# Phase 1 of a fused attention and two-MLP kernel: four engines pinned to the text's order, the attention cut into a table of half units

## Chip, core and metric

One core of a Trainium2 chip runs the whole program. The metric is the device time of one execution in microseconds; lower is better.

## What is computed

```python
# q, k, v: 8 batches x 8 heads x 576 positions x 64; together 4608 tokens of 512 columns
q_s = exp(q - max(q, -1));  q_s /= sum(q_s, -1) + 1e-9
k_s = exp(k - max(k, 2));   k_s /= sum(k_s, 2) + 1e-9
x = einsum(q_s, einsum(k_s, v))                  # linear attention, then heads to columns
x = relu(x @ w_in) ** 2 @ w_out                  # phase 1: 512 -> 2048 -> 512
xn = x / sqrt(mean(x * x) + 1e-6) * rms_g        # phase 2: 512 -> 1536 -> 512
out = (silu(xn @ w_gate) * (xn @ w_val)) @ w_out2
```

The weights come as 64-bit floats and are converted on the chip.

## The kernel before

**Tiles.** The 4608 tokens are nine blocks of 512 (`NB`). Phase 1 goes over the blocks, and in each over sixteen chunks of 128 of the 2048 hidden columns (`FF1`). One block and chunk (j, c) is a **unit**. Every matmul operand is split into a high and a low part, so that a product is three matmuls (`PASSES`): high times high, high times low, low times high.

**A unit** is twelve matmuls into `ps_h` (`p1_h`, through `mm3`, L107), then on ACT a Relu (L625), a Square (L626) and the copy of the high part (L78), on DVE the subtraction that leaves the low part (L79, `g<-r,g`), and two units later (`LAG`) twelve matmuls into the four accumulators `acc` (`p1_B`, L107). The first product of the second half of block 1's chunks is made in block 0 already (`kept`, `AHEAD`), so that the second eight units of block 1 have only the `acc` matmuls. The last unit of a block is followed by four copies of `acc` to `e` (L663 on DVE, L665 on ACT) and four stores.

**The attention** of the next block runs beside these units, one pair of heads (`hp`, four of them) after the other. For each pair PE makes a transpose `ps_kt` (L453), a second one `ps_kb` (L464), four transposes `ps_q` (L540), twenty small matmuls `ps_kv` (L558) and six matmuls `ps_x` (L107). All five take their bank from two (`a0`, `a1`, in turn): the next one can start when the tile before the last has been read.

```python
return ps_a.tile([P, 512], F32, tag=f"a{turns['a'] % 2}", name=name)   # a_ps
```

Between them stand DVE and ACT steps: the maximum over k (`mk`, L441 and L444), `mc` and `mcb` out of `ps_kt` (L455, L457; `ps_kb` transposes `mcb`), the subtraction from k out of `ps_kb` (L474), its exponential `ke` (L494), the same for q (`qm` L503, `qt` L510, L514), its sum and quotient (`qs` L518 to L520, `qn` L527), the high and low part of `qT` out of `ps_q`, `rk` and `kvf` out of `ps_kv` (L574 to L578), and the two parts of `kvd` and of `x`, the latter out of `ps_x`. The parts go through `split`: high on ACT (L78), low on DVE (L79).

**Weights.** Those of phase 1 are converted during block 0, and written to DRAM but for eight tiles; a ring of seven tiles (`ws`) is filled again from there by SP. Those of phase 2 are converted in blocks 2 to 6, by `tick`: a load of 64-bit words (`raw`), a word on POOL (`s<-raw`, L242) and one on ACT (L245), three instructions on DVE (L257, L265, L269, called a **conversion** below), then sums (L329) and low parts (L274) on POOL, the high part on ACT (L273), and a store that ACT's queue issues.

**Order.** The text gives each unit its products, then the ticks that are due, then the attention steps that `A_STEPS` and `A_STARTS` put on this unit. Most instructions may be moved by the scheduler of the program's layer, engine by engine, by priority; only those wrapped in `held` keep their place in the text (the first instruction of each PE step of the attention, and the high parts on ACT).

Of the kernel before, what the change touches and what calls it, by code (L numbers as in the profile page):

```python
# [22 lines left out]

@with_exitstack
def attention_moe_kernel(
# [12 lines left out]
    nc = tc.nc  # L38
    B, H, S, D = q.shape
# [34 lines left out]
    def held(j, ins):  # L74
        return tc.keep_in_program_order(ins) if j > 0 else ins

    def split(dst, src, j=0):
        held(j, nc.scalar.activation(out=dst[:, 0], in_=src, func=AF.Copy))  # L78
        nc.vector.tensor_tensor(  # L79
            out=dst[:, 1], in0=src, in1=dst[:, 0].bitcast(F32), op=ALU.subtract  # L80
        )

    def split_by_pe(dst, ps, j):
        held(j, nc.scalar.activation(out=dst[:, 0], in_=ps, func=AF.Copy))
        nc.tensor.matmul(ps, neg_r, dst[:, 0], start=False, stop=True, skip_group_check=True)
# [147 lines left out]
    def d_words(key):  # L233
# [5 lines left out]
        if key[0] in ("i", "o"):  # L239
            nc.scalar.activation(out=s, in_=hi, func=AF.Copy, scale=2.0**-112)  # L240
        else:
            nc.gpsimd.tensor_scalar(  # L242
                out=s, in0=hi, scalar1=2.0**-112, scalar2=0.0, op0=ALU.mult, op1=ALU.add
            )
        nc.scalar.activation(out=n, in_=r[:, :, 0], func=AF.Copy, scale=2.0**-29)  # L245
        words[key] = s, n

    def d_float(key):
# [8 lines left out]
        nc.vector.tensor_scalar(  # L257
# [7 lines left out]
        nc.vector.scalar_tensor_tensor(  # L265
# [15 lines left out]
    def flush(all=False):  # L281
        for x in late:
            x[0] -= 1
        while late and (late[0][0] < 0 or all):
            _, key, t = late.pop(0)
            if key[0] not in PROD:
                tc.keep_in_program_order(nc.scalar.dma_start(out=wd[key], in_=flat(t)))
                continue
            for g in range(2):
# [3 lines left out]
                    nc.scalar.dma_start(  # L293
# [24 lines left out]
    def d_quad(key):  # L318
# [7 lines left out]
        def d_sum(name, in0, in1, op):  # L326
            def run():
                f[name] = pools["q"].tile([P, 512], F32, tag=name, name=name, bufs=1)
                nc.gpsimd.tensor_tensor(out=f[name], in0=f[in0], in1=f[in1], op=op)  # L329
# [90 lines left out]
    def a_loadv(j, hp):  # L420
# [4 lines left out]
        nc.gpsimd.memset(vt[:, :, :, D : D + 1], 1.0)  # L425
# [10 lines left out]
    def a_kmax(j, hp):  # L436
# [23 lines left out]
    def a_kb(j, hp):  # L460
# [3 lines left out]
        held(j, nc.tensor.transpose(ps[:, 0:P], mcs.pop((j, hp)), ident))  # L464
        mcs[j, hp] = ps

    def a_ksub(j, hp):
# [4 lines left out]
        for rows, cs in k_parts:  # L472
            n = cs.stop - cs.start
            nc.vector.tensor_tensor(  # L474
# [12 lines left out]
    def a_kexp(j, hp):  # L487
# [5 lines left out]
        for rows, cs in k_parts:  # L493
            ins = nc.scalar.activation(out=ke[rows, cs], in_=kv_[rows, cs], func=AF.Exp)  # L494
# [6 lines left out]
    def a_qmax(j, hp):  # L501
        qm = pools["a"].tile([P, 2 * NG], F32, tag="qm", name="qm")
        nc.vector.reduce_max(out=qm, in_=q_heads(j, hp), axis=AX.X)  # L503
        qms[j, hp] = qm

    def a_qsub(j, hp):
        qv = q_heads(j, hp)
        qm = qms.pop((j, hp)).unsqueeze(2).to_broadcast([P, 2 * NG, D])
        eng = nc.vector if j > 0 else nc.gpsimd
        eng.tensor_tensor(out=qv, in0=qv, in1=qm, op=ALU.subtract)  # L510

    def a_qexp(j, hp):
        qv = q_heads(j, hp)
        held(j, nc.scalar.activation(out=qv, in_=qv, func=AF.Exp))  # L514

    def a_qsum(j, hp):
        qs = pools["a"].tile([P, 2 * NG], F32, tag="qs", name="qs")
        nc.vector.reduce_sum(out=qs, in_=q_heads(j, hp), axis=AX.X)  # L518
        nc.vector.tensor_scalar_add(out=qs, in0=qs, scalar1=1e-9)
        nc.vector.reciprocal(out=qs, in_=qs)  # L520
        qms[j, hp] = qs

    def a_qn(j, hp):
# [3 lines left out]
        nc.vector.tensor_tensor(  # L527
# [7 lines left out]
    def a_qT(j, hp):  # L535
        ps = a_ps(j, hp, "ps_q")
        qt = qns.pop((j, hp))
        for c in range(NG):
            src = qt[:, c].rearrange("p h d -> p (h d)")
            ins = nc.tensor.transpose(ps[:, c * P : (c + 1) * P], src, ident)  # L540
            if c == 0:
                held(j, ins)
        qT = a_tile(j, hp, [2, T], "qT", F32R)
# [4 lines left out]
        qTs[j, hp] = qT  # L548

    def a_kv(j, hp):  # L550
# [18 lines left out]
    def a_kvd(j, hp):  # L569
        if j >= B:  # L570
# [15 lines left out]
        split(kvd[j % 2][hp], f, j)  # L586
# [5 lines left out]
    def a_x(j, hp):  # L592
        ps = a_ps(j, hp, "ps_x")
        qT = qTs.pop((j, hp))
        xts[j, hp] = xp.tile([P, 2, T], F32R, tag="x", name="x")
# [15 lines left out]
        if j < 2:  # L611
            split_by_pe(xts[j, hp], ps, j)
        else:
            split(xts[j, hp], ps, j)
# [5 lines left out]
    def p1_h(j, c, pool, bufs):  # L620
        ps = ps_h.tile([P, T], F32, tag="h", name="ps_h")
        for kk in range(KD):
            mm3(ps, wl(("i", c), kk), lambda b: xts[j, kk][:, b, :], kk == 0, kk == KD - 1)
        r = pool.tile([P, T], F32, tag="r", name="r", bufs=bufs)
        nc.scalar.activation(out=r, in_=ps, func=AF.Relu)  # L625
        nc.scalar.activation(out=r, in_=r, func=AF.Square)  # L626
        return r

    def p1_A(j, c):
        if ahead(j, ("i", c)):  # L630
            r = kept.pop(c)
        else:
            r = p1_h(j, c, gp, 2)
# [17 lines left out]
    def p1_B(j, c):  # L651
# [7 lines left out]
        if c == FF1 - 1:  # L659
# [426 lines left out]
```

## Time and profile before

| | |
|---|---|
| Median of 3 runs | 1773.79 us (1771.77 to 1775.23) |
| The profiled execution | 1773.63 us, of it the profile's span 1771.5 us |
| PE busy | 1718.5 us, 97% of the span |
| DVE, ACT, POOL busy | 1086.5 us (61%), 761.8 us (43%), 154.9 us (9%) |
| Chain that ended last | PE 71%, DMA 4%, DVE, POOL and ACT 1% each |

The span is that of the instructions on the core; some 2 us of the execution lie outside it. Busy time is the sum of the instructions' own times. PE overlaps matmuls, so a group of twelve is best read from the start of one group to the start of the next.

### The profile page before, as it was taken

What the parts mean: (1) busy time and instruction counts of PE and PEld (TensorE: products, weight loads), DVE (VectorE), ACT (ScalarE), POOL (GpSimd) and SP (SyncE); (2) the same over time, 40 slices, a digit from 0 to 9 for tenths busy, and PEclk for the clock granted to TensorE, in tenths of its full rate; (3) what the DMA queues carried; (4) which work ended last, traced back from release to release, by engine and by line L of the source; (5) the groups of instructions that cost most, each with busy time, mean ns of one, the idle gap of its engine ahead of it and who ended that gap; (6) DMA issues with size and microseconds to landing.
All of it is one profiled execution on the core that took longest, in us unless ns stands there. A gap on an engine that the chain in (4) does not pass through costs nothing.

```text
span 1771.5 us, 22992 instructions
## 1 busy us (share of the span) xinstructions
PE 1718.5 (97%) x8338; PEld 1417.2 (80%) x8338; DVE 1086.5 (61%) x1866; ACT 761.8 (43%) x1351; POOL 154.9 (9%) x166
## 2 busy tenths in 40 slices
PE   5899998999998999999999999999999999999998
PEld 3678877887886888888888888888888888888997
DVE  7987576555587445332275777667757775756444
ACT  5677435444555444443445334423442343223221
POOL 2000035013165002010000000000000000000000
PEclk9999998999999999999999999999999999999999
DMA  6788658678799557565556557666666566666885
GB/s 184 242 276 287 217 190 282 209 226 291 221 369 314 181 185 238 168 206 194 190 166 226 191 190 252 202 212 200 236 216 216 192 215 219 199 209 195 287 298 204
DMA packets 184511, 398.41 MB, mean 225 GB/s; under 512 B 57424, under 2 KB 96336, under 8 KB 183248
## 3 DMA queue, kind: packets, MB, share of 16 engines
q1 hardware_dynamic: 156368, 356.05, 61.5%
q10 hardware_dynamic: 28032, 40.90, 6.4%
q8 instruction: 67, 1.10, 0.3%
q14 instruction: 44, 0.36, 0.1%
HBM read 337.12 MB, written 59.77 MB: 224 GB/s over the span
## 4 chain that ended last, share of the span: by engine, by line
PE 71%; DMA 4%; DVE 1%; POOL 1%; ACT 1%; issue 0%; SPq 0%; ACTq 0%; POOLq 0%
PE acc L107 28%; PE ps_h L107 12%; PE ps_y L792 8%; PE ps_v L792 8%; PE ps_x L792 8%; PE ps_w L792 4%; DMA wd_t<-so 1%; DMA raw<-in_w_gv 1%; PE ps_x L107 1%; DMA ws<-wd_o 1%; PE ps_kv L558 1%; DMA wd_u<-so 0%; POOL so L274 0%; PE ps_q L540 0%; DMA raw<-in_w_out 0%
## 5 line engine op out<-in xcount | busy, mean ns | idle before, releaser
L107 PE MATMUL ps_h<-x,ws 128*128 128x512 f32 x1296 | 326.5, 402 | 4.0 <-DVE ws L274 2.6
L107 PE MATMUL acc<-g,ws 128*128 128x512 f32 x1296 | 313.9, 391 | 1.6 <-DVE g L79 1.1
L107 PE MATMUL acc<-ws,g 128*128 128x512 f32 x1296 | 313.4, 390 | 1.0 <-ACT g L78 0.9
L79 DVE TENSOR_TENSOR g<-r,g 128x512 fp32r<-128x512 f32 x252 | 180.0, 714 | 214.0 <-ACT g L78 212.0
L107 PEld LDWEIGHTS ps_h<-x,ws 128*128 128x128 f32 x1296 | 242.1, 191 | 58.2 <-DVE ws L274 3.9
L107 PEld LDWEIGHTS acc<-g,ws 128*128 128x128 f32 x1296 | 243.2, 188 | 54.3 <-DVE g L79 2.0
L107 PEld LDWEIGHTS acc<-ws,g 128*128 128x128 f32 x1296 | 241.4, 188 | 51.4 <-ACT g L78 2.1
L78 ACT ACTIVATE g<-r 128x512 fp32r<-128x512 f32 x252 | 158.8, 630 | 252.7 <-DVE r L831 225.7
L625 ACT ACTIVATE r<-ps_h 128x512 f32<-128x512 f32 x144 | 85.3, 593 | 212.2 <-PE ps_h L107 202.8
L792 PE MATMUL ps_y<-xo,ws 128*128 128x512 f32 (+1 forms) x720 | 168.7, 369 | 0.0
L792 PE MATMUL ps_v<-xo,ws 128*128 128x512 f32 (+1 forms) x720 | 168.5, 368 | 0.0
L792 PE MATMUL ps_x<-xo,ws 128*128 128x512 f32 (+1 forms) x720 | 167.4, 368 | 0.0
L792 PEld LDWEIGHTS ps_x<-xo,ws 128*128 128x128 f32 x720 | 128.0, 188 | 23.5
L792 PEld LDWEIGHTS ps_v<-xo,ws 128*128 128x128 f32 x720 | 127.7, 188 | 23.4
L792 PEld LDWEIGHTS ps_y<-xo,ws 128*128 128x128 f32 x720 | 126.4, 189 | 24.2 <-DVE sa L704 1.5
L107 PE MATMUL ps_h<-x,w 128*128 128x512 f32 x432 | 110.0, 402 | 1.7 <-DVE w L274 0.9
L107 PE MATMUL acc<-g,w 128*128 128x512 f32 x432 | 104.2, 390 | 1.0 <-ACT w L273 1.0
L107 PEld LDWEIGHTS ps_h<-x,w 128*128 128x128 f32 x432 | 80.6, 192 | 20.5 <-DVE w L274 1.3
L107 PEld LDWEIGHTS acc<-g,w 128*128 128x128 f32 x432 | 80.9, 188 | 18.3 <-ACT w L273 1.4
L626 ACT ACTIVATE r<-r 128x512 f32<-128x512 f32 x144 | 90.0, 629 | 12.8 <-POOL so L274 8.7
L808 DVE TENSOR_TENSOR u<-ps_y,p 128x512 f32<-128x512 f32 (+1 forms) x120 | 76.1, 634 | 23.3 <-PE ps_y L792 21.6
L819 ACT ACTIVATE sg<-silu 128x512 f32<-128x512 f32 (+1 forms) x90 | 51.4, 585 | 81.4 <-DVE silu L808 78.8
(113 smaller groups left out, 1852.8 us busy)
## 6 DMA issues: line engine op xcount, KB each, us to landing
ws<-wd_t SPq DMA_DIRECT2D x210, 512.0 KB, 4.1
ws<-wd_u SPq DMA_DIRECT2D x108, 512.0 KB, 4.2
ws<-wd_o SPq DMA_DIRECT2D x96, 512.0 KB, 4.1
ws<-wd_i SPq DMA_DIRECT2D x89, 512.0 KB, 4.2
wd_t<-so ACTq DMA_DIRECT2D x84, 256.0 KB, 5.0
raw<-in_w_out SPq DMA_DIRECT2D x28, 512.0 KB, 5.2
raw<-in_w_gv SPq DMA_DIRECT2D x24, 512.0 KB, 6.0
x2d<-e SPq DMA_DIRECT2D x36, 256.0 KB, 3.2
```

The lines of the kernel that those rows point to most:

```text
L78: held(j, nc.scalar.activation(out=dst[:, 0], in_=src, func=AF.Copy))
L79: nc.vector.tensor_tensor(out=dst[:, 1], in0=src, in1=dst[:, 0].bitcast(F32), op=ALU.subtract)
L107: ins = nc.tensor.matmul(ps, lhsT(a), rhs(b), start=first and n == 0, stop=last and n == 2, skip_group_check=part,)
L558: ins = nc.tensor.matmul(ps[h * D : (h + 1) * D, 0 : D + 1], ke[0:m, c, h, :], vt[0:m, c, h, :], start=c == 0, stop=c == SF,)
L625: nc.scalar.activation(out=r, in_=ps, func=AF.Relu)
L626: nc.scalar.activation(out=r, in_=r, func=AF.Square)
L792: nc.tensor.matmul(ps, w[:, q % 2, o : o + P], x(xa, kk), start=first and kk == 0 and m == 0, stop=last and kk == 1 and m == 2, skip_group ...
L808: nc.vector.tensor_tensor(out=out, in0=in0, in1=in1, op=ALU.add)
L819: nc.scalar.activation(out=g, in_=h, func=AF.Sigmoid)
```

## The change

From the second block to the last but one (`FF1 <= i < n1 - FF1`, 112 of the 144 units) every instruction of VectorE, ScalarE, GpSimd and TensorE is kept in the text's order: `ve`, `se`, `ge` and `te` wrap the engines and do this while `pinned[0]` is set. SP's queue is not wrapped. The text of these units is written anew:

- A unit has two halves. The first is the `ps_h` matmuls of unit i, then ACT's Relu, Square and high part of unit i-1, then the attention steps of half 2i. The second is the `acc` matmuls of unit i-2, DVE's low part of unit i-1, the tick and one POOL output if due, then the steps of half 2i+1.
- The attention of blocks 2 to 8 is the table `HALVES`: 23 steps, each with its half relative to the pair's start; pairs follow each other every eight halves. `split` is cut into `split_hi` (ACT) and `split_lo` (DVE), which have a half each, and so have `a_kt` and `a_mc`, `a_kb` and `a_ksub`, `a_kv` and `a_kvf`. Block 1's attention stays as it was.
- The copies of `acc` to `e` (`p1_out`) move to the third unit of the next block, ahead of its attention steps; that unit has no `acc` matmuls, as before, and the fourth has two sets.

No instruction is added or left out: on each engine there are as many of each kind as before. Block 8 and phase 2 have the order that they had.

```diff
+class InOrder:
+    def __getattr__(self, name):
+        f = getattr(self.engine, name)
+        def call(*args, **kw):
+            ins = f(*args, **kw)
+            return self.tc.keep_in_program_order(ins) if self.on[0] else ins
+        return call
...
+    ve, se, ge, te = (
+        InOrder(tc, engine, pinned) for engine in (nc.vector, nc.scalar, nc.gpsimd, nc.tensor)
+    )
...
-    A_STEPS = ((-5, a_loadk), (-4, a_loadq), (0, a_qmax), (0, a_kmax), (1, a_qsub), (1, a_ktr))
-    A_STEPS += ((3, a_kbs), (2, a_qexp), (3, a_loadv), (3, a_qsum), (4, a_kexp))
-    A_STEPS += ((4, a_qn), (6, a_kvn), (6, a_qT), (8, a_x))
-    A_STARTS = {1: (-6, -4, -2, 0), 2: (-6, -3, 0, 3)}
...
+    HALVES = ((-12, a_loadk), (-10, a_loadq), (-3, a_kmax), (-2, a_qmax), (0, a_qsub))
+    HALVES += ((0, a_loadv), (2, a_qexp), (3, a_kt), (3, a_qsum), (4, a_mc), (4, a_qn))
+    HALVES += ((6, a_kb), (7, a_ksub), (8, a_kexp), (8, a_qT), (9, a_qT_hi), (10, a_qT_lo))
+    HALVES += ((10, a_kv), (11, a_kvf), (12, a_kvd_hi), (13, a_kvd_lo), (14, a_x))
+    HALVES += ((15, a_x_hi), (16, a_x_lo))
...
+                    at += (j - 1) * 2 * FF1 - 11 + 2 * FF1 // NP * hp
...
+            pinned[0] = FF1 <= i < n1 - FF1
...
             p1_A(j, c)
+            if not pinned[0]:
+                p1_hi(j, c)
+                p1_lo(j, c)
+            for x in last:
+                p1_hi(*x)
+            if pinned[0] and c == LAG:
+                p1_out(j - 1)
+            attention(2 * i)
             pending.append((j, c, None))
             while len(pending) > (LAG + 1 if j > 0 and c == LAG else LAG):
                 p1_B(*pending.pop(0)[:2])
+            for x in last:
+                p1_lo(*x)
+            last = [(j, c)] if pinned[0] else []
             while ticks[0] < n_ticks(i):
                 tick()
             if i > 2 * FF1 and outs:
                 outs.pop(0)()
...
-            for n, ja, hp, f in todo.get(i, ()):
-                f(ja, hp)
+            attention(2 * i + 1)
```

**Where the order moves.** PE at the start of block 2 (`w_655` is a resident tile of the second unit's weights), before:

```order
L540 MATMUL ps_q<-ident,qn 128x128 x4
L558 MATMUL ps_kv<-vt,ke 64x65 x10
L107 MATMUL ps_h<-x,w_655 128x512 x12
L107 MATMUL acc_2102<-g,w_1944 128x512 x3
L107 MATMUL acc_2103<-g,w_1944 128x512 x3
L107 MATMUL acc_2104<-g,w_1944 128x512 x3
L107 MATMUL acc_2105<-g,w_1944 128x512 x3
L464 MATMUL ps_kb<-ident,mcb 128x128
L107 MATMUL ps_h<-x,ws 128x512 x12
L107 MATMUL ps_x<-qT,kvd_0_84 128x4x48 x3
```

and with the change (all lines of wrapped calls read L34):

```order
L34 MATMUL ps_h<-x,w_655 128x512 x12
L34 MATMUL acc_2100<-g,w_1961 128x512 x3
L34 MATMUL acc_2101<-g,w_1961 128x512 x3
L34 MATMUL acc_2102<-g,w_1961 128x512 x3
L34 MATMUL acc_2103<-g,w_1961 128x512 x3
L34 MATMUL ps_x<-qT,kvd_0_84 128x4x48 x3
L34 MATMUL ps_x<-qT,kvd_0_88 128x4x80 x3
L34 MATMUL ps_kb<-ident,mcb 128x128
L34 MATMUL ps_h<-x,ws 128x512 x12
L34 MATMUL ps_q<-ident,qn 128x128 x4
L34 MATMUL ps_h<-x,ws 128x512 x12
```

`ps_q` and `ps_kv` stood between `ps_kt` and `ps_kb` and took the two banks; now `ps_x` and `ps_kb` follow each other behind the `acc` group, and `ps_q` stands one unit later.

DVE in block 2 before, from the step after `mcb` to the first read of `ps_kv` (`t` is a weight under conversion):

```order
L269 ISA t_3179<-t_3179,n 128x1024
L265 SCALAR_TENSOR_TENSOR t_3296<-s,t_3296 128x512
L257 TENSOR_SCALAR t<-s 128x512
L269 ISA t_3296<-t_3296,n 128x1024
L265 SCALAR_TENSOR_TENSOR t<-s,t 128x512
L257 TENSOR_SCALAR t<-s 128x512
L269 ISA t<-t,n 128x1024
L265 SCALAR_TENSOR_TENSOR t<-s,t 128x512
L79 TENSOR_TENSOR g<-r,g 128x512
L269 ISA t<-t,n 128x1024
L79 TENSOR_TENSOR qT<-ps_q,qT 128x512
L574 TENSOR_SCALAR rk<-ps_kv 128x1
```

and with the change, in the same block, from the step ahead of `ps_kb`'s reader to the first read of `ps_kv`:

```order
L34 TENSOR_REDUCE qm<-qt 128x8
L34 TENSOR_TENSOR kt<-kt,ps_kb 128x2x256
L34 TENSOR_TENSOR kt<-kt,ps_kb 64x2x64
L34 TENSOR_TENSOR g<-r,g 128x512
L34 TENSOR_TENSOR x<-ps_x,x 128x512
L34 TENSOR_TENSOR qt<-qt,qm 128x512
L34 TENSOR_TENSOR g<-r,g 128x512
L34 TENSOR_SCALAR t_3072<-s 128x512
L34 SCALAR_TENSOR_TENSOR t_3072<-s,t_3072 128x512
L34 ISA t_3072<-t_3072,n 128x1024
L34 TENSOR_TENSOR qT<-ps_q,qT 128x512
L34 TENSOR_SCALAR rk<-ps_kv 128x1
```

Before, instructions of four conversions stood ahead of the low part of `qT`; now one conversion at most stands between two attention steps. Where a conversion is due in the third unit of a block, DVE has it between `ps_kb`'s reader and the low part of `x` (here in block 3):

```order
L34 TENSOR_TENSOR kt<-kt,ps_kb 128x2x256
L34 TENSOR_TENSOR kt<-kt,ps_kb 64x2x64
L34 TENSOR_TENSOR g<-r,g 128x512
L34 TENSOR_SCALAR t_3714<-s 128x512
L34 SCALAR_TENSOR_TENSOR t_3714<-s,t_3714 128x512
L34 ISA t_3714<-t_3714,n 128x1024
L34 TENSOR_TENSOR x<-ps_x,x 128x512
L34 TENSOR_TENSOR qt<-qt,qm 128x512
```

The low part of `x` empties the bank that the next `ps_q` takes.

## Rows read from the trace of the kernel before

**Rows 1.** Stretches: length, busy PE, PEld, DVE, ACT, POOL, PEclk, DMA share, GB/s
```profile
180.00:760.00 580.00, 562.87 (x2916) 460.77 (x2915) 340.59 (x628) 276.62 (x503) 137.83 (x131) 0.99 0.73 239
760.00:1771.00 1011.00, 1005.93 (x4669) 839.39 (x4667) 597.81 (x934) 364.17 (x618) 4.56 (x4) 1.00 0.64 213
```

**Rows 2.** PE's waits, 180 to 760 us: total us, times, longest
```profile
PE ps_kb L464 <- DVE rk L574: 5.4, 2, 3.9
PE ps_kb L464 <- DVE qT L79: 3.7, 1, 3.7
PE ps_kb L464 <- DVE rk L575: 3.4, 1, 3.4
PE ps_kv L558 <- DVE mc L455: 2.8, 3, 1.6
PE acc L107 <- DVE g L79: 1.1, 2, 1.0
PE ps_h L107 <- DVE x L79: 0.8, 1, 0.8
```

**Rows 3.** Stretches, 180 to 760 us, in which PE was idle
```profile
250.00:310.00 60.00, 51.89 (x249) 41.95 (x248) 44.22 (x72) 29.99 (x56) 35.29 (x30) 0.91 0.81 269
...
410.00:440.00 30.00, 26.05 (x130) 20.98 (x129) 17.34 (x30) 14.14 (x26) 7.31 (x8) 0.94 0.87 298
...
510.00:575.00 65.00, 59.92 (x317) 47.68 (x316) 54.38 (x86) 36.99 (x68) 37.77 (x34) 1.00 0.96 339
```

**Rows 4.** Timeline of PE (start us, us): twelve matmuls after a wait
```profile
265.92 5.47 PE L107 MATMUL ps_h<-x,ws 128*128 128x512 f32 x12
...
297.81 4.31 PE L107 MATMUL ps_h<-x,ws 128*128 128x512 f32 x12
...
425.36 4.58 PE L107 MATMUL ps_h<-x,ws 128*128 128x512 f32 x12
...
553.68 3.01 PE L107 MATMUL ps_h<-x,w 128*128 128x512 f32 x12
```

**Rows 5.** Timeline of PE without waits, 323 to 331 us
```profile
323.75 0.27 PE L464 MATMUL ps_kb<-ident,mcb 128*128 128x128 f32 x1
...
326.60 2.88 PE L107 MATMUL acc<-g,w 128*128 128x512 f32 x12
329.32 0.94 PE L107 MATMUL ps_x<-qT,kvd 128*128 128x192 f32 x6
330.10 2.88 PE L107 MATMUL ps_h<-x,ws 128*128 128x512 f32 x12
```

**Rows 6.** Timeline of DVE, 254 to 263 us: two conversions
```profile
254.09 0.41 DVE L257 TENSOR_SCALAR t<-s 128x512 uint32<-128x512 uint32 x1
254.43 0.67 DVE L269 CUSTOM_DVE_ANT_0 t<-t,n 128x1024 uint16<-128x1024 uint16 x1
255.03 0.67 DVE L265 SCALAR_TENSOR_TENSOR t<-s,t 128x512 uint32<-128x512 uint32 x1
257.51 1.50 DVE L257 TENSOR_SCALAR t<-s 128x512 uint32<-128x512 uint32 x1 [1.81 <-POOL s L242]
258.94 1.78 DVE L269 CUSTOM_DVE_ANT_0 t<-t,n 128x1024 uint16<-128x1024 uint16 x1
260.64 1.78 DVE L265 SCALAR_TENSOR_TENSOR t<-s,t 128x512 uint32<-128x512 uint32 x1
```

**Rows 7.** Timeline of POOL, 257 to 261 us
```profile
257.45 1.28 POOL L329 TENSOR_TENSOR s<-t,t 128x512 f32<-128x512 f32 x1
258.69 1.47 POOL L274 TENSOR_TENSOR so<-t,so 128x512 fp32r<-128x512 f32 x1
```

**Rows 8.** Timeline of DVE, 347 to 372 us: single steps
```profile
347.55 0.69 DVE L79 TENSOR_TENSOR g<-r,g 128x512 fp32r<-128x512 f32 x1 [1.05 <-ACT g L78]
348.42 0.88 DVE L474 TENSOR_TENSOR kt<-kt,ps_kb 128x512 f32<-128x512 f32 x2 [0.18 <-PE ps_kb L464]
...
355.30 0.69 DVE L79 TENSOR_TENSOR x<-ps_x,x 128x512 fp32r<-128x512 f32 x1 [1.48 <-ACT x L78]
...
371.32 0.69 DVE L663 COPY e<-acc 128x512 f32<-128x512 f32 x1 [0.45 <-PE acc L107]
```

More of the change, by code (lines that the diff above doesn't have):

```diff
@@ L74, in held @@
     def held(j, ins):
-        return tc.keep_in_program_order(ins) if j > 0 else ins
+        return tc.keep_in_program_order(ins) if j > 0 and not pinned[0] else ins
     def split(dst, src, j=0):
-        held(j, nc.scalar.activation(out=dst[:, 0], in_=src, func=AF.Copy))
-        nc.vector.tensor_tensor(
+        held(j, se.activation(out=dst[:, 0], in_=src, func=AF.Copy))
+        ve.tensor_tensor(
             out=dst[:, 1], in0=src, in1=dst[:, 0].bitcast(F32), op=ALU.subtract
@@ L328, in run @@
                 f[name] = pools["q"].tile([P, 512], F32, tag=name, name=name, bufs=1)
[L329 removed]
+                ge.tensor_tensor(out=f[name], in0=f[in0], in1=f[in1], op=op)
             outs.append(run)
@@ L493, in a_kexp @@
         for rows, cs in k_parts:
-            ins = nc.scalar.activation(out=ke[rows, cs], in_=kv_[rows, cs], func=AF.Exp)
+            ins = se.activation(out=ke[rows, cs], in_=kv_[rows, cs], func=AF.Exp)
             held(j, ins)
@@ L569, in a_kvd, with a_kvd_hi, a_kvd_lo, a_kvf @@
     def a_kvd(j, hp):
+        a_kvf(j, hp)
+        if j < B:
+            split(kvd[j % 2][hp], kvs.pop((j, hp)), j)
+    def a_kvd_hi(j, hp):
+        if j < B:
+            split_hi(kvs, (j, hp), kvd[j % 2][hp])
+    def a_kvd_lo(j, hp):
+        if j < B:
+            split_lo(kvs, (j, hp))
+            kvs.pop((j, hp))
+    def a_kvf(j, hp):
         if j >= B:
@@ L585, in a_kvd @@
         )
-        split(kvd[j % 2][hp], f, j)
+        kvs[j, hp] = f
     def a_kvn(j, hp):
@@ L623, in p1_h, with p1_r, p1_hi, p1_lo @@
             mm3(ps, wl(("i", c), kk), lambda b: xts[j, kk][:, b, :], kk == 0, kk == KD - 1)
+        return ps
+    def p1_r(ps, pool, bufs):
         r = pool.tile([P, T], F32, tag="r", name="r", bufs=bufs)
-        nc.scalar.activation(out=r, in_=ps, func=AF.Relu)
-        nc.scalar.activation(out=r, in_=r, func=AF.Square)
+        se.activation(out=r, in_=ps, func=AF.Relu)
+        se.activation(out=r, in_=r, func=AF.Square)
         return r
     def p1_A(j, c):
[L630 to L633, printed above, removed]
+        if not ahead(j, ("i", c)):
+            kept[j, c] = p1_h(j, c)
+            if j == 0:
+                kept[j, c] = p1_r(kept[j, c], gp, 2)
         if j == 0 and c >= AHEAD:
-            kept[c] = p1_h(1, c, pools["r"], FF1 - AHEAD)
+            kept[1, c] = p1_r(p1_h(1, c), pools["r"], FF1 - AHEAD)
         if not ahead(j, ("i", c)):
             used(("i", c))
-        g = g_tile(c % 4)
-        split(g, r)
-        ghl[1, j, c] = g
+    def p1_hi(j, c):
+        r = kept.pop((j, c))
+        if j > 0 and not ahead(j, ("i", c)):
+            r = p1_r(r, gp, 2)
+        ghl[1, j, c] = r
+        split_hi(ghl, (1, j, c), g_tile(c % 4))
+    def p1_lo(j, c):
+        split_lo(ghl, (1, j, c))
     kept = {}
@@ L658, in p1_B, with p1_out @@
         used(("o", c))
-        if c == FF1 - 1:
-            for m in range(KD):
-                e = ep.tile([P, T], F32, tag="e", name="e")
-                if m % 2:
-                    nc.vector.tensor_copy(out=e, in_=acc[m])
-                else:
-                    nc.scalar.activation(out=e, in_=acc[m], func=AF.Copy)
-                nc.sync.dma_start(out=x2d[j][:, m, :], in_=e)
+        if c == FF1 - 1 and not pinned[0]:
+            p1_out(j)
+    def p1_out(j):
+        for m in range(KD):
+            e = ep.tile([P, T], F32, tag="e", name="e")
+            if m % 2:
+                ve.tensor_copy(out=e, in_=acc[m])
+            else:
+                se.activation(out=e, in_=acc[m], func=AF.Copy)
+            nc.sync.dma_start(out=x2d[j][:, m, :], in_=e)
     x2s, sums, rinv = {}, {}, {}
@@ L983, in attention_moe_kernel, with attention @@
                     f(0, int(step[1]))
-        for i in sorted(todo):
-            if i < 0:
-                for n, j, hp, f in todo[i]:
-                    f(j, hp)
+        def attention(at):
+            for n, j, hp, f in todo.get(at, ()):
+                f(j, hp)
+        for at in sorted(todo):
+            if at < 0:
+                attention(at)
         pending = []
-        tasks = {}
+        last = []
         for i, (j, c) in enumerate(units):
```

182 lines of the change are left out of this document (110 added, 72 removed).

## Prediction, made before the changed kernel was run

> **What bounds it now.** I read the stretches first. PE was busy for 1005.93 of the 1011 us after 760 us, and for 562.87 of the 580 us from 180 to 760 us [rows 1]. The latter are the units that the change touches: 17.1 us of PE's idle time lie there, beside 340.59 us of DVE and 276.62 us of ACT, so no other engine is near its limit over the whole stretch. Behind 760 us the order stays. Then I read PE's waits of this stretch [rows 2]: six rows, 17.2 us together, and the releaser is DVE in each. 12.5 us are `ps_kb`, late for a bank that DVE had not emptied yet (`rk`, `qT`). No DMA and no ACT stands there. The third view is where PE stood still: three stretches of 60, 30 and 65 us [rows 3], in which POOL is busy up to 35.29 of 60 us. The fourth shows a second price of a wait. Twelve matmuls behind the three long waits took 5.47, 4.31 and 4.58 us, against 3.01 us behind a short one [rows 4]; the granted clock of their stretches is 0.91 and 0.94, and 1.00 in the third [rows 3]: after the long waits PE ran for some matmuls at the lower of its two levels, 1.2 instead of 2.4 GHz. That is 2.5 + 1.3 + 1.6 = 5.4 us.
>
> So the waits cost 17.2 + 5.4 = **22.6 us**, and this is all there is to be had: in the clean stretch a group of 12 starts 2.7 to 2.85 us after the group before it [rows 5], and the change takes no matmul away.
>
> Why was DVE late? At 257.51 us a conversion's three instructions took 1.50, 1.78 and 1.78 us, one after the other, and had waited 1.81 us for POOL; three instructions just ahead took 0.41, 0.67 and 0.67 us [rows 6]. Four conversions were lined up before the low part of `qT`, which holds the bank.
>
> **What the change removes.** `ps_kb` now stands one and a half units behind `ps_kt`, its `mc` and `mcb` are the first attention steps of DVE behind `ps_kt`, and `ps_q` and `ps_kv` are no longer between the two. `ps_kv`'s wait for `mc` goes for the same reason: `mc` has two units. Conversions come singly, at most one a unit. I count all 22.6 us as gone.
>
> **What it adds.** The new tight place is `ps_q`: it takes the bank of `ps_x`, which DVE's low part of `x` empties in the very half in which `ps_q` stands. From `ps_kb` on, PE has the `ps_h` and the `acc` group before `ps_q`, 329.32 - 323.75 = 5.57 us; in a block's third unit, without `acc`, 326.60 - 323.75 = 2.85 us [rows 5]. DVE in this time: 0.27 us for `ps_kb` [rows 5] and 0.18 us until it is seen, 0.88 us for the subtraction, 0.69 for a `g`, 0.69 for `x` [rows 8], together **2.7 us**. A conversion between them adds 0.41 + 0.67 + 0.67 = 1.75 us, or 1.50 + 1.78 + 1.78 = 5.06 us when it meets POOL [rows 6]. There are 27 `ps_q` in the pinned units (four in each of blocks 1 to 6, three in block 7). In the order, eight have a conversion in between: two in a third unit (blocks 3 and 6), six in ordinary units.
>
> - Two third units with a conversion: 2.7 + 1.75 = 4.45 us, against 2.85 us: 1.6 us late. Ends: never late, and 2.7 + 5.06 - 2.85 = 4.9 us late with 1.6 us of lowered clock behind it (4.58 - 3.01 us [rows 4]). Two times: 0 to 13.0; I take the plain conversion, 3.2 us.
> - Five third units without one: 2.7 against 2.85 us would do, but two copies of `acc` (0.69 us each [rows 8]) stand ahead of the subtraction and start with `ps_x`, which takes 330.10 - 329.32 = 0.78 us [rows 5]; so DVE begins up to 0.6 us late. 0 to 0.5 us each; I take 0.1, 0.5 us together.
> - Six ordinary units with one: 4.45 against 5.57 us, not late. Meeting POOL, 7.76 us: 2.2 late. POOL is busy 137.83 of 580 us [rows 1], a quarter, and more where conversions are; I take two of six, 4.4 us. Ends 0 and 13.2.
> - Block 1's second eight units: there PE has one group between `ps_kb` and `ps_q`, 2.85 us, and no conversion on DVE's side: 2.7 us, on the edge. With the end of block 0, whose order moves too: I take 0.5 us; ends 0 and 3.9, the longest wait of PE [rows 2].
> - Nothing else is costed, and what hides it: the low part of `g` has two groups of slack (its `acc` is two units behind); `kvd`'s low part stands a full group ahead of `ps_x`; the `acc` copies are due only in the fourth unit. ACT's three instructions a unit are unchanged, and it has 276.62 of 580 us of work [rows 1]. POOL in order: the `vt` fill and the word of a weight come a tick before DVE needs it. SP is not pinned, its queue only sees releases in another order; loads of k and q stand eight halves or more ahead of their readers. If DVE fell behind by a unit, `g` would be late next.
>
> Sum: -22.6 + 3.2 + 0.5 + 4.4 + 0.5 = **-14.0 us**. The profiled execution took 1773.63 us, of it 1771.5 in the span, and stands 0.2 us from the median of 1773.79 us. So **1759.6 us**. With all ends low 1751.0, with all ends high 1773.63 - 22.6 + 13.0 + 2.5 + 13.2 + 3.9 = 1783.6; the POOL end would need all eight conversions to collide, so I give the forecast 1751 to 1769.
>
> While that conversion ran slowly, POOL was in instructions of 1.28 and 1.47 us [rows 7], and 1.5 to 1.8 us are little less than a plain one and such a neighbour together. The Trainium skill, "SBUF — State Buffer", section "Who interferes with whom", says why: DVE and GpSimd share one pair of ports under an exclusive lock, and a DVE instruction with two SBUF inputs, or in a two-port mode, blocks fully against a GpSimd instruction that reads SBUF. By it the same text that puts the conversion and POOL's output into one half would make every conversion at a `ps_q` a slow one; the rows show both kinds, the fast one 3 us ahead of the slow one, so I do not take it for all eight.
>
> **Rivals.**
>
> *Every conversion collides.* POOL's output of a unit stands right behind the tick in the text, and the engines meet each time. For it: the slow rows. Against it: POOL's three quarters of idle time. Then 2 x (4.9 + 1.6) + 6 x 2.2 + 0.5 + 0.5 = 27.2 us against 22.6: 1778.2 us, no gain. This is the rule named above as a time of its own. Chance 0.10.
>
> *The wait moves to ps_q everywhere (the other side).* DVE now may not run anything ahead of a head that waits, for POOL, ACT or a load; before, its list was arranged for what was ready. If it reaches each low part of `x` late, all 27 `ps_q` wait. The price is a wait of the present size, 17.2 us over ten times [rows 2], 1.7 us: 27 x 1.7 = 46 us, less 22.6: 1797 us. It decides from (22.6 + 3.5) / 27 = 0.97 us each. For it: one bank, one half. Against it: 2.7 against 5.57 us where no conversion stands, and DVE's 340.59 of 580 us. Chance 0.13.
>
> *The transfers were behind the third stretch.* From 510 to 575 us the DMA share is 0.96 at 339 GB/s [rows 3]; if words and `ws` come late there, those 5.1 us stay, and the sum is -8.9: 1764.7 us. Against it: PE's waits name DVE alone. Chance 0.12.
>
> **Numbers.** The forecast has 0.65. About 0.2% (3.5 us) is what a measurement of this kernel can tell from no change: faster ends at 1770.2, slower begins at 1777.3 us. Faster: 0.65 less 0.02, and 0.12: 0.75. Same: these 0.02 and half of the first rival's 0.10 with 0.01 of the second's: 0.08. Slower: 0.05 and 0.12: 0.17. The range, 1750 to 1774, holds the forecast and the transfers, and leaves out 0.2, nearly all of it above.
>
> **What would show it.** Right: between 180 and 745 us no wait of PE at `ps_kb`; PE's waits there below 10 us and most at `ps_q`, released by DVE's `x`, the longest in the third units of blocks 3 and 6; no group of 12 above 3.1 us outside them; the same busy times of DVE, ACT and POOL within a few per cent. Wrong: waits at `ps_q` in units without a conversion, waits at `g`, or a PE wait released by ACT, POOL or a DMA.

## The result and the profile after

The changed kernel takes **1755.96 us** (median of 4 runs, 1755.16 to 1756.29), the kernel before 1773.05 us (4 runs on the same chip); the ratio is 0.9902, 95% interval 0.9885 to 0.9919. So it is faster by 17 us; the forecast was 14.0 us, 1759.6. The profiled execution took 1756.28 us, its span 1754.3 us.

The page's busy times and its chain that ended last, of which PE holds 94% instead of 71%:

```profile
PE 1713.2 (98%) x8338; PEld 1412.2 (81%) x8338; DVE 1065.3 (61%) x1866; ACT 766.4 (44%) x1351; POOL 151.3 (9%) x166
...
PE 94%; DVE 3%; DMA 1%; issue 1%; ACT 1%; SPq 0%; POOL 0%; ACTq 0%; DVEq 0%; POOLq 0%
```

The stretches that answer to [rows 1]; the units of blocks 1 to 7 now end at about 745 us instead of 760 (columns: length, busy time of PE, PEld, DVE, ACT, POOL, granted clock, DMA share, GB/s):

```profile
180.00:745.00 565.00, 560.27 (x2930) 458.66 (x2929) 320.24 (x632) 281.67 (x504) 128.47 (x126) 1.00 0.77 244
745.00:1754.00 1009.00, 1003.12 (x4654) 836.88 (x4652) 600.98 (x934) 364.39 (x619) 12.11 (x9) 1.00 0.64 214
```

PE is idle for 4.7 of 565 us, before for 17.1 of 580 [rows 1]. Its waits of the stretch, where [rows 2] had six rows and 17.2 us, are one row (total, times, longest):

```profile
PE ps_q L34 <- DVE x L34: 4.7, 3, 3.3
```

All six old waits are gone, and the new one has the place and the releaser that were named. The longest of the three, in block 3's third unit, on PE, DVE and POOL (start, duration, engine, instruction, idle time before it and what ended it):

```profile
366.95 0.63 PE L34 MATMUL ps_q<-ident,qn 128*128 128x128 f32 x4 [3.28 <-DVE x L34]
367.33 4.58 PE L34 MATMUL ps_h<-x,ws 128*128 128x512 f32 x12
...
362.38 0.41 DVE L34 TENSOR_SCALAR t<-s 128x512 uint32<-128x512 uint32 x1
362.83 1.70 DVE L34 SCALAR_TENSOR_TENSOR t<-s,t 128x512 uint32<-128x512 uint32 x1
364.56 1.64 DVE L34 CUSTOM_DVE_ANT_0 t<-t,n 128x1024 uint16<-128x1024 uint16 x1
366.13 0.68 DVE L34 TENSOR_TENSOR x<-ps_x,x 128x512 fp32r<-128x512 f32 x1
...
362.69 1.29 POOL L34 TENSOR_TENSOR so<-s,so 128x512 fp32r<-128x512 f32 x1 [6.32 <-ACT so L34]
363.92 0.12 POOL L34 MEMSET vt<- 128x10 f32 x1
363.98 1.68 POOL L34 TENSOR_TENSOR s<-t,s 128x512 f32<-128x512 f32 x1
365.63 1.09 POOL L34 TENSOR_SCALAR s<-raw 128x512 f32<-128x512 f32 x1
```

The conversion meets two instructions of POOL; behind the wait twelve matmuls take 4.58 us instead of 3.01 [rows 4], at a granted clock of 0.66 from 367 to 372 us. The other two waits are 1.29 us (block 6's third unit, a conversion that met nothing) and 0.16 us. So the change adds 4.7 us of waits and 1.6 us of lowered clock. With the 22.6 us that went, that is 16.3 of the 17.2 us of the span.

The rest is clock. The prediction priced it by the twelve matmuls right behind a wait, but the lower level reached further: at 301.92 us the next twelve still took 3.20 us, and at 271.18 us `ps_x` took 1.25 us instead of the 0.94 of [rows 5]. Ten us from each of the three places of before, then the one of the change (columns as above):

```profile
265.00:275.00 10.00, 9.21 (x32) 7.60 (x33) 9.52 (x20) 5.56 (x11) 6.45 (x7) 0.66 0.53 183
297.00:307.00 10.00, 9.32 (x37) 7.72 (x38) 7.39 (x15) 6.02 (x12) 3.21 (x3) 0.83 0.62 216
425.00:435.00 10.00, 9.74 (x39) 8.01 (x40) 6.90 (x16) 6.31 (x12) 0.12 (x1) 0.83 0.91 307
...
367.00:377.00 10.00, 10.00 (x40) 8.14 (x40) 1.70 (x3) 4.17 (x7) 1.29 (x1) 0.83 0.68 234
```

What is missing from the full clock there is, as an estimate, 3.4 + 1.7 + 1.7 = 6.8 us before, not 5.4, and 1.7 us with the change. Then waits and clock together give 12.5 + 5.1 = 17.6 us, and the span's 17.2 us are accounted for.

So far the prediction seems right but for sizes. The experiments show that its reason for the 22.6 us was at most a part of it.

### The profile page after: what moved, and what is told of

The parts are those of the page before. It is cut to its first block, busy times and chain, and to the rows that moved or that the text cites. A ratio compares the mean times of both kernels' runs of the same rounds, so it can differ in the third digit from the quotient of the medians.

```text
span 1754.3 us, 22975 instructions
## 1 busy us (share of the span) xinstructions
PE 1713.2 (98%) x8338; PEld 1412.2 (81%) x8338; DVE 1065.3 (61%) x1866; ACT 766.4 (44%) x1351; POOL 151.3 (9%) x166
## 4 chain that ended last, share of the span: by engine, by line
PE 94%; DVE 3%; DMA 1%; issue 1%; ACT 1%; SPq 0%; POOL 0%; ACTq 0%; DVEq 0%; POOLq 0%
PE acc L34 38%; PE ps_h L34 21%; PE ps_x L34 10%; PE ps_y L34 8%; PE ps_v L34 8%; PE ps_w L34 4%; PE ps_kv L34 2%; PE ps_q L34 1%; DVE t L34 1%; DMA vt<-in_v 1%; DVE mk L34 0%; DVE kt L34 0%; DVE qs L34 0%; DMA x2d<-e 0%; DMA kt<-in_k 0%
## 5 line engine op out<-in xcount | busy, mean ns | idle before, releaser
L34 PE MATMUL ps_h<-x,ws 128*128 128x512 f32 x1296 | 322.2, 398 | 4.0 <-DVE ws L34 2.6
L34 PE MATMUL acc<-g,ws 128*128 128x512 f32 x1296 | 315.2, 392 | 0.4 <-DVE ws L34 0.4
L34 PE MATMUL acc<-ws,g 128*128 128x512 f32 x1296 | 313.4, 390 | 1.0 <-ACT g L34 0.9
L34 PEld LDWEIGHTS ps_h<-x,ws 128*128 128x128 f32 x1296 | 240.9, 190 | 56.2 <-DVE ws L34 3.9
L34 PEld LDWEIGHTS acc<-g,ws 128*128 128x128 f32 x1296 | 241.9, 188 | 52.8 <-DVE ws L34 1.5
L34 PEld LDWEIGHTS acc<-ws,g 128*128 128x128 f32 x1296 | 241.4, 188 | 51.3 <-ACT g L34 2.1
L34 ACT ACTIVATE g<-r 128x512 fp32r<-128x512 f32 x252 | 158.7, 631 | 230.5 <-DVE r L34 226.0
L34 DVE TENSOR_TENSOR g<-r,g 128x512 fp32r<-128x512 f32 x252 | 172.5, 684 | 122.0 <-ACT g L34 120.3
L34 ACT ACTIVATE r<-ps_h 128x512 f32<-128x512 f32 x144 | 85.8, 597 | 243.0 <-PE ps_h L34 239.8
L34 PE MATMUL ps_y<-xo,ws 128*128 128x512 f32 (+1 forms) x720 | 168.6, 369 | 0.0
L34 PE MATMUL ps_v<-xo,ws 128*128 128x512 f32 (+1 forms) x720 | 168.4, 368 | 0.0
L34 PE MATMUL ps_x<-xo,ws 128*128 128x512 f32 (+1 forms) x720 | 167.5, 368 | 0.5 <-ACT p L34 0.5
L34 PEld LDWEIGHTS ps_x<-xo,ws 128*128 128x128 f32 x720 | 127.9, 188 | 24.4 <-ACT p L34 0.9
L34 PEld LDWEIGHTS ps_v<-xo,ws 128*128 128x128 f32 x720 | 127.7, 188 | 23.4
L34 PEld LDWEIGHTS ps_y<-xo,ws 128*128 128x128 f32 x720 | 126.4, 189 | 24.2 <-DVE sa L34 1.5
L34 PE MATMUL ps_h<-x,w 128*128 128x512 f32 x432 | 109.4, 402 | 0.9 <-DVE w L34 0.9
L34 PE MATMUL acc<-g,w 128*128 128x512 f32 x432 | 104.9, 392 | 1.0 <-ACT w L34 1.0
L34 PEld LDWEIGHTS ps_h<-x,w 128*128 128x128 f32 x432 | 81.2, 192 | 18.5 <-DVE w L34 1.3
L34 PEld LDWEIGHTS acc<-g,w 128*128 128x128 f32 x432 | 80.5, 188 | 18.7 <-ACT w L34 1.4
L34 ACT ACTIVATE r<-r 128x512 f32<-128x512 f32 x144 | 90.2, 631 | 3.7
L34 DVE TENSOR_TENSOR u<-ps_y,p 128x512 f32<-128x512 f32 (+1 forms) x120 | 76.0, 633 | 23.0 <-PE ps_y L34 21.5
L34 ACT ACTIVATE sg<-silu 128x512 f32<-128x512 f32 (+1 forms) x90 | 51.5, 585 | 83.6 <-DVE silu L34 83.4
```

What stands on the lines that cost most here:

```text
L34: ins = f(*args, **kw)
```

## Experiments

Each kernel was timed over five rounds beside the kernel before on the same chip; the ratios are to that.

### Three ways to take the new wait away

The first edit:

```diff
-        at = [n for n in range(2 * FF1 + 1, i + 1) if n % FF1 >= 2]
+        at = [n for n in range(2 * FF1 + 1, i + 1) if n % FF1 >= 3]
```

The second:

```diff
-    HALVES += ((15, a_x_hi), (16, a_x_lo))
+    HALVES += ((15, a_x_lo), (15, a_x_hi))
```

`both` has the two together. Of two steps of one half, the one listed later is issued first, so the high part still precedes the low one.

> Edit: no conversion in a block's third unit any more (units with c >= 3 instead of c >= 2 are counted for the ticks), the rest as in the changed kernel. Theory 'bank late by a conversion': PE's only long waits in the pinned units, 3.28 us in block 3's third unit and 1.29 us in block 6's, are there because a conversion stands on DVE between ps_kb and the low part of x; both vanish, with the 1.9 us of lowered clock behind the longer one: about 6.5 us less, 1749.5 us. Rival 'third unit tight by itself' (ps_x, ps_kb and ps_q within one group of twelve): the waits stay at 1 us or more in third units without a conversion, 1754 to 1756 us. Rival 'conversion meets POOL elsewhere': new waits of over 1 us at ps_q in ordinary units, where the conversions now stand, 1753 us or more.

> Edit: DVE's low part of x one half unit earlier, ahead of the subtraction from k, of g and of the conversion. Theory 'bank late by a conversion': nothing of the tick stands between ps_x and the release of its bank, so no wait at ps_q is left in any unit, whether a conversion is there or not: 1749 to 1750 us. Rival 'ACT late': the low part of x now waits for ACT's high part at DVE's head, and holds up the subtraction, g and the conversion behind it: waits at ps_kv or acc of 0.5 us and more in many units, 1756 us or more.

> Both edits (no conversion in third units, low part of x a half earlier). Theory 'bank late by a conversion': either edit alone takes the same 6.5 us away, so together they give what each gives, 1749 to 1750 us. Rival 'two causes' (tight third unit and collisions elsewhere): together more than each alone, each alone 1752 to 1754 us.

Measured: 1749.41 us (ratio 0.9867, interval 0.9844 to 0.9889), 1747.53 us (0.9855, 0.9833 to 0.9878) and 1747.37 us (0.9855, 0.9833 to 0.9878); the last two are some 2 us below what was expected. (The 1.9 us of lowered clock that the expectations name are 1.6 to 1.7 us by the rows above.) In none of the three has PE a wait left from 180 to 745 us, and PE is busy for all of it; the stretch with the early low part of `x` (columns as above):

```profile
180.00:745.00 565.00, 565.00 (x2961) 463.47 (x2960) 329.32 (x634) 285.30 (x508) 129.99 (x127) 1.00 0.75 246
```

The conversion between `ps_kb` and the low part of `x` was the cause of the new wait; a third unit without one does not wait, and in these kernels an ordinary unit with one loses nothing. Moving one subtraction half a unit forward gives 8 us over the changed kernel. The two kernels with it, 1747.5 and 1747.4 us, are the fastest of the study; whether the 2 us to the first of the three are real is left open, for the profiles of the first and the second have the same span (1746.4 us).

### POOL taken away from the conversion, and more conversions

POOL taken away (`third` is a flag that starts as `[False]`):

```diff
-        if key[0] in ("i", "o"):
+        if key[0] in ("i", "o") or third[0]:
...
+            third[0] = c == LAG
...
-            if i > 2 * FF1 and outs:
-                outs.pop(0)()
+            n_out = {1: 0, LAG: 0, LAG + 1: 3}.get(c, 1) if j in (3, 6) else 1
+            for n in range(n_out):
+                if i > 2 * FF1 and outs:
+                    outs.pop(0)()
```

> Edit: the changed kernel, but in the third units of blocks 3 and 6 POOL has nothing to do (word of the weight on ACT, the outputs of the second and third unit given with the fourth's); the conversion stays where it is. Theory 'POOL makes the conversion slow': block 3's conversion takes about 0.4, 0.7 and 0.7 us instead of 0.41, 1.70 and 1.64, its wait at ps_q falls from 3.28 us to about that of block 6 (1.3), and the lowered clock behind it goes: 2 + 1.9 us less, 1752 us. Rival 'late for another reason' (acc copies, or DVE behind since block 2): the wait and 1756 us stay.

Measured: 1752.73 us (0.9883, 0.987 to 0.9896), as expected to 0.7 us. The same place, block 3's third unit:

```profile
365.33 0.63 PE L34 MATMUL ps_q<-ident,qn 128*128 128x128 f32 x4 [1.32 <-DVE x L34]
365.71 3.01 PE L34 MATMUL ps_h<-x,ws 128*128 128x512 f32 x12
...
362.71 0.41 DVE L34 TENSOR_SCALAR t<-s 128x512 uint32<-128x512 uint32 x1
363.16 0.69 DVE L34 SCALAR_TENSOR_TENSOR t<-s,t 128x512 uint32<-128x512 uint32 x1
363.89 0.69 DVE L34 CUSTOM_DVE_ANT_0 t<-t,n 128x1024 uint16<-128x1024 uint16 x1
```

With POOL idle the two slow instructions take 0.69 us each instead of 1.70 and 1.64, PE waits 2.0 us less, and the granted clock stays at 1.00 from 365 to 370 us (3.01 us for the twelve matmuls). So POOL made the conversion slow, at 1.0 us an instruction. The Trainium skill, "SBUF — State Buffer", section "Who interferes with whom", has the rule: a DVE instruction with two inputs in SBUF contends with a GpSimd instruction that reads SBUF. The trace agrees: the two instructions that suffer here read two tiles of SBUF, while `x<-ps_x,x`, with one input in PSUM, took 0.68 us at 366.13 us, beside a POOL instruction that ran from 365.63 to 366.72 us. Two inputs are not the only case, though: in [rows 6] `t<-s`, with one input, took 1.50 us instead of 0.41 beside POOL.

More conversions:

```diff
-        at = [n for n in range(2 * FF1 + 1, i + 1) if n % FF1 >= 2]
-        return min(NJ1 + 4 + len(at) * 11 // 20, len(jobs) + 4)
+        at = [n for n in range(2 * FF1 + 1, i + 1) if n % FF1 in (2, 4, 6, 8, 10, 12, 14)]
+        return min(NJ1 + 4 + len(at), len(jobs) + 4)
```

> Edit: seven ticks a block at even units instead of 11 in 20, so that 20 conversions instead of 8 stand between ps_kb and the low part of x: four in third units (blocks 3 to 6, two before) and 16 in ordinary ones (six before). The conversions reach into block 7. Theory 'the third unit is tight, an ordinary one is not': from 1749.5 us without any, four times the 1.3 us of block 6 up to four times block 3's 3.3 + 1.9 us, 1755 to 1770 us, all waits at ps_q in third units. Rival 'every collision costs' (the forecast's term for ordinary units, 2 of 6 at 2.2 us): 16 x 0.73 = 12 us more, 1767 to 1782 us, with waits at ps_q in ordinary units.

Measured: 1765.81 us (0.9957, 0.9945 to 0.9969). PE waits 11.2 us at `ps_q`, in six places: 3.29, 2.29, 2.26 and 2.26 us in the four third units, and twice some 0.5 us in the 16 ordinary ones. Two of the shorter ones with what follows:

```profile
467.12 0.63 PE L34 MATMUL ps_q<-ident,qn 128*128 128x128 f32 x4 [2.29 <-DVE x L34]
467.50 2.98 PE L34 MATMUL ps_h<-x,ws 128*128 128x512 f32 x12
...
670.09 0.84 PE L34 MATMUL ps_q<-ident,qn 128*128 128x128 f32 x4 [2.26 <-DVE x L34]
670.58 4.50 PE L34 MATMUL ps_h<-x,ws 128*128 128x512 f32 x12
```

Nearly the same wait once leaves the clock at 1.00 and once is followed by 0.66 (670 to 675 us). Over the four third units the lowered clock adds 4.4 us in the twelve matmuls behind the waits (4.58, 2.98, 4.25 and 4.50 us against 2.98). The third unit is tight and the ordinary one hardly: the term "six ordinary units, two of six at 2.2 us" was set far too high.

### Which engine's order counts

The text and the table stay; only the engines that are kept in the text's order differ (`[False]` in place of `pinned` for the others; the instructions that the kernel before held are held).

```diff
-        InOrder(tc, engine, pinned) for engine in (nc.vector, nc.scalar, nc.gpsimd, nc.tensor)
+        InOrder(tc, engine, on)
+        for engine, on in (
+            (nc.vector, [False]), (nc.scalar, [False]), (nc.gpsimd, [False]), (nc.tensor, [False])
+        )
```

> Edit: the changed text and table, but the four engines are not pinned in these units: the scheduler orders DVE, ACT and POOL as in the kernel before (first PE instruction of an attention step and the high parts on ACT keep their place). PE's order is the changed kernel's but for a few single instructions; DVE again has up to seven conversion instructions one behind the other, some ahead of the low parts of x and qT. Theory 'DVE's order counts': PE waits at ps_q, ps_kv or ps_kb again, released by DVE behind such a bunch, 8 to 20 us in the stretch, 1762 to 1774 us. Rival 'bank distance counts' (PE's new order gives each bank its time, whatever DVE does first): at most 3 us from the changed kernel, 1753 to 1759 us.

Measured: 1783.03 us (1.0056, 1.0036 to 1.0076), slower than the kernel before and above both expected ranges. PE's wait and the most of ACT's waits for a store, 180 to 760 us:

```profile
PE ps_q L34 <- DVE x L34: 24.6, 7, 10.5
...
ACT so L34 <- DMA wd_t<-so: 16.5, 9, 6.3
```

So the table, with PE's order all but word for word that of the change, moves the wait from `ps_kb` to `ps_q`, the place that the second rival named, and makes it larger. Without any pinning the new text gains nothing. Which engine's pinning counts? I took DVE's.

> Edit: the changed text and table, DVE alone pinned in these units; PE, ACT and POOL go back to the scheduler (with the instructions held that were held before). Theory 'DVE's order counts': the 24.6 us at ps_q that came back without any pinning go again, for DVE's row is the changed kernel's word for word: 1754 to 1759 us. Rival 'an order on all four counts' (DVE at a head that waits for ACT or POOL, which now do other things first): waits at ps_q or acc stay, 1765 us or more.

> Edit: the changed text and table, PE, ACT and POOL pinned, DVE left to the scheduler; up to four conversion instructions stand ahead of a low part of x. Theory 'DVE's order counts': waits at ps_q of 8 to 25 us, 1764 to 1783 us. Rival 'POOL and ACT count' (DVE bunches conversions because POOL delivers words in bunches): 1754 to 1759 us.

Measured: DVE alone 1766.95 us (0.9965, 0.9951 to 0.9979), all but DVE **1750.32 us** (0.9872, 0.9857 to 0.9887). The second is below both expected ranges. My theory fell: DVE's order is neither enough nor needed, though pinned alone it takes 16 us off the time of the table alone. Left to the scheduler, DVE even has no conversion between the reader of `ps_kb` and the low part of `x` (0 of 23 places from 180 to 760 us, counted from the trace, against 8 in the change). That can be why the kernel is faster than the change, but it isn't what keeps PE from waiting: the table without any pinning has 0 of 23 as well. With DVE alone pinned, PE's waits, 180 to 760 us:

```profile
PE ps_q L34 <- DVE x L34: 12.2, 5, 5.6
```

and the timeline of ACT and DVE at the longest of them, which ends at 650 us:

```profile
640.04 0.63 ACT L34 ACTIVATE r<-r 128x512 f32<-128x512 f32 x1
645.15 0.63 ACT L34 ACTIVATE so<-t 128x512 fp32r<-128x512 f32 x1 [4.48 <-DMA wd_t<-so]
645.69 0.61 ACT L34 ACTIVATE g<-r 128x512 fp32r<-128x512 f32 x1
646.21 0.58 ACT L34 ACTIVATE x<-ps_x 128x512 fp32r<-128x512 f32 x1
...
646.34 1.39 DVE L34 TENSOR_TENSOR g<-r,g 128x512 fp32r<-128x512 f32 x1 [6.19 <-ACT g L34]
```

An instruction at the front of its engine's queue, its **head**, holds up all that stands behind it. ACT stands 4.48 us in front of a weight's output, because its tile `so` is still being stored; the high parts of `g` and `x` are queued behind it, DVE's low parts wait for those (`g<-r,g` for 6.19 us), behind that one the conversion and the low part of `x` are queued, and PE waits for the bank. The Trainium skill, "PSUM — Partial Sum Buffer", section "Engine vs sequencer instructions", calls ACT's, DVE's and GpSimd's queues strict first-in-first-out, and these rows agree. That gave a new theory:

> Edit: the changed text and table, ACT alone pinned. The theory 'DVE's order counts' has fallen (all but DVE pinned: 1750.3 us; DVE alone: 1767 us). New theory 'ACT's list': left to the scheduler, ACT takes copies of weights (so) ahead of the high parts of g and x and then waits at its head for a store to land (4.48 us at 640.67 us with DVE alone pinned), and the bank of ps_x is emptied late. Then pinning ACT alone gives about what all but DVE gives: 1749 to 1755 us. Rival 'POOL's list' (words and outputs in bunches make DVE's bunches): 1762 us or more here.

> Edit: the changed text and table, POOL alone pinned. Theory 'ACT's list': the waits at ps_q stay, 10 us or more, 1762 to 1783 us. Rival 'POOL's list': 1749 to 1755 us.

Measured: ACT alone **1749.31 us** (0.9864, 0.9849 to 0.988), POOL alone 1775.64 us (1.0018, 1.0004 to 1.0032). With ACT pinned there is no wait of PE and no wait of ACT for a store from 180 to 760 us, although DVE then stands longer in front of conversions, waiting for POOL, than in the kernel before (31.7 us in this stretch against 13.5). With POOL pinned both kinds of wait are there:

```profile
PE ps_q L34 <- DVE x L34: 20.4, 9, 3.8
...
ACT so L34 <- DMA wd_t<-so: 27.6, 15, 5.5
```

### The old text with pinned engines

`before_pin_act_pool` and `before_pin_all` are the kernel before, with its text and its `A_STEPS`, and only this added, beside the wrapper `InOrder` (here the first; in the second all four read `pinned`):

```diff
+    ve, se, ge, te = (
+        InOrder(tc, engine, on)
+        for engine, on in (
+            (nc.vector, [False]), (nc.scalar, pinned), (nc.gpsimd, pinned), (nc.tensor, [False])
+        )
+    )
...
+            pinned[0] = FF1 <= i < n1 - FF1
```

> Edit: the kernel before, its text and its steps, with ACT and POOL pinned from the second block to the last but one; DVE and PE left to the scheduler as before. Theory 'weights in bunches' (the 17.2 us at ps_kb and the other banks came from outputs and conversions that the lists put ahead of the steps which empty banks; the table has no part in the gain): the waits go, 1748 to 1756 us. Rival 'the table counts' (ps_q and ps_kv between ps_kt and ps_kb take both banks): 8 us and more of waits at ps_kb, 1762 us or more.

> Edit: the kernel before, its text and its steps, with all four engines pinned from the second block to the last but one. Theory 'weights in bunches': any order that spreads the weights does, and so does this one where the low part of x and the conversions have a unit each: 1748 to 1758 us. Rival 'the table counts': the old steps, a whole unit each, put DVE's head behind ACT's in every unit, waits at ps_kb, ps_q and acc, above 1765 us.

Measured: **1748.29 us** (0.986, 0.9847 to 0.9874) and **1749.33 us** (0.9867, 0.9853 to 0.988). All that is left of [rows 2] in the first:

```profile
PE ps_kb L34 <- DVE rk L34: 0.8, 1, 0.8
```

So the gain does not need the table. The old steps with ACT and POOL in the text's order are 7.7 us better than the changed kernel, and equal to the one with the early low part of `x` (1747.5 us) within what a measurement of this kernel can tell.

What the pinned order of ACT changes, its starts show. The text gives at most one weight output a unit; the 54 copies to `so` go through four tiles in turn. In the kernel before, a copy and the fourth after it are as close as 12.6 us, in the changed one never closer than 23.0 us (counted from the trace), and no copy there waits for its tile. It is so in every run: in the ten kernels with ACT pinned the two are never closer than 21.1 us and no copy waits for a store, in the four without (before, table alone, DVE alone, POOL alone) they come as close as 10.4 to 15.8 us, and 10 to 25 copies wait between 180 and 760 us. ACT's waits for weight tiles in the kernel before, 180 to 760 us:

```profile
ACT so L273 <- DMA wd_t<-so: 21.4, 13, 3.5
ACT n L245 <- DVE t L269: 15.7, 7, 3.8
ACT so L273 <- DMA wd_u<-so: 8.5, 5, 3.8
```

and its timeline of ACT, DVE and PE at the third long wait at `ps_kb`:

```profile
419.05 0.61 ACT L626 ACTIVATE r<-r 128x512 f32<-128x512 f32 x1
422.03 0.63 ACT L273 ACTIVATE so<-s 128x512 fp32r<-128x512 f32 x1 [2.37 <-DMA wd_u<-so]
422.57 0.61 ACT L78 ACTIVATE g<-r 128x512 fp32r<-128x512 f32 x1
423.09 0.58 ACT L78 ACTIVATE qT<-ps_q 128x512 fp32r<-128x512 f32 x1
...
423.21 1.39 DVE L79 TENSOR_TENSOR g<-r,g 128x512 fp32r<-128x512 f32 x1 [1.77 <-ACT g L78]
424.53 0.68 DVE L79 TENSOR_TENSOR qT<-ps_q,qT 128x512 fp32r<-128x512 f32 x1
425.13 0.14 DVE L574 TENSOR_SCALAR rk<-ps_kv 128x1 f32<-128x1 f32 x1
...
425.26 0.37 PE L464 MATMUL ps_kb<-ident,mcb 128*128 128x128 f32 x1 [3.95 <-DVE rk L574]
```

PE's row says "`ps_kb` waits for DVE's `rk`". Two engines further back stands a store of a weight that only phase 2 needs.

This is the chain behind one of the four waits at `ps_kb`, not behind all. At the second, DVE itself stands at its head for 4.43 us, in front of a conversion, and ACT for 2.39 us in front of its `g`; by the profile POOL ends both waits. The longest wait of the table alone (10.47 us) comes in the same way, from DVE's head and POOL, while its second (7.42 us) has ACT's store again (6.27 us, up to 563 us). Before, then the table alone:

```profile
294.29 0.43 DVE L257 TENSOR_SCALAR t<-s 128x512 uint32<-128x512 uint32 x1 [4.43 <-POOL so L274]
294.67 0.63 ACT L78 ACTIVATE g<-r 128x512 fp32r<-128x512 f32 x1 [2.39 <-POOL vt L425]
297.68 0.30 PE L464 MATMUL ps_kb<-ident,mcb 128*128 128x128 f32 x1 [3.37 <-DVE rk L575]
...
303.37 1.47 DVE L34 TENSOR_SCALAR t<-s 128x512 uint32<-128x512 uint32 x1 [7.40 <-POOL so L34]
306.37 1.09 PE L34 MATMUL ps_q<-ident,qn 128*128 128x128 f32 x4 [10.47 <-DVE x L34]
```

At the first and the fourth (3.70 us at 265.79 and 1.45 us at 553.60) DVE has not waited since 257.51 and 545.11 us: it works, through conversions among other things, at the first place beside POOL [rows 6, 7]. Nor do ACT's waits for stores measure PE's: with DVE alone pinned they are 63.8 us and PE's 13.0, in the table alone 19.4 and 24.9. That ACT's order decides is shown by the runs; that its stand in front of stores is how it does so is shown at some of the waits and argued for the rest. The test of it, the scheduler's order with more than four tiles for `so`, was not run.

## Why the prediction was right, and where its reason was not

- **What bounds it.** Right: the old waits and their lowered clock were nearly all there was, and they went whole. The kernels without a wait end 1.6 to 3.7 us below 1773.63 - 22.6 = 1751.0 us; 1.4 us of that is the clock, which cost some 6.8 us and not 5.4. The -22.6 came close because it is the whole of the waits in the trace, whatever takes them away; it says nothing for the reason that was given.
- **"Why was DVE late?"** This step took one place for all. The prediction read PE's releaser (DVE), then DVE's own row at the first long wait, a line of conversions with POOL beside it [rows 6, 7], and stopped: "No DMA and no ACT stands there". For that place the reading holds. At the second DVE stood 4.43 us for POOL, at the third ACT stood 2.37 us for a store, and neither was looked up. ACT's waits of 45.6 us for weight tiles (21.4, 15.7 and 8.5) were in the trace of before.
- **"What the change removes."** This step failed. The distance from `ps_kt` to `ps_kb` and the single conversions were named as the reasons. The table without pinning is 9.5 us slower than the kernel before, the old text with ACT and POOL pinned 25 us faster. In the new text ACT's order alone takes all of PE's waits away, DVE's and POOL's alone do not (13.0 and 20.4 us are left).
- **What it adds.** The place (`ps_q`), the releaser (`x`) and the two units were right. The sizes were not: two third units 3.2 forecast, 4.6 of waits and 1.6 of clock measured, since one of the two met POOL; ordinary units 4.4 forecast, 0.16 measured (a conversion that waited 1.47 us for POOL); third units without a conversion 0.5 and block 1 with the end of block 0 0.5, nothing measured. Together 8.6 against 6.3 us.
- **The rivals.** "Every conversion collides" and the transfers did not come. "The wait moves to `ps_q` everywhere" did not come either, but the place is right for the table without pinning: 24.6 us in seven places, though there DVE is not kept in order, which was that rival's reason.

Open: whether ACT alone is enough on the old text (it ran together with POOL), and how much of ACT's part is its own stand in front of stores and how much the words and copies that it hands to DVE and POOL.

## What to carry to other kernels

A row that says "PE waits for DVE" names the last link. Ask of the releaser what it waited for, and go on until an engine stands at its own head, and do it for each long wait, not for one: here it was ACT in front of a copy whose tile had not been stored at one, DVE in front of a conversion at another. In a queue that serves the critical path, keep background work (weights, stores) spread out and behind the urgent steps: in the new text, pinning ACT alone gave all of the gain that four pinned engines gave, and more (1749.31 against 1755.96 us).

## What the runs showed of the hardware

A conversion instruction that meets POOL takes 1.64 to 1.70 us instead of 0.69; with POOL's work moved away from that place, the same conversion took 0.69 us. And a wait of 2.3 us is followed by the full clock at one place (granted 1.00, twelve matmuls in 2.98 us) and by the lower one at another (0.66, 4.50 us), so the lowered clock behind a wait of this size has no fixed price. Behind one of the waits of before it outlasted twelve matmuls: the next group, at 301.92 us, still took 3.20 us instead of 2.88 [rows 5].
